# A fused adaLN, linear-attention and SwiGLU block: later modulation rows on VectorE instead of TensorE

## The chip, the cores and the metric

The kernel runs on one core of a Trainium2 chip. The metric is the device time of one execution in microseconds (us), the median over several runs. All times below are in us unless marked ns.

A core has a matrix engine (TensorE, PE in the profile, with its weight loads shown apart as PEld), a vector engine (VectorE, DVE), a scalar engine for activations (ScalarE, ACT), a general engine (GpSimd, POOL) and an engine that issues transfers (SyncE, SP). Each executes its own instructions in order and waits on semaphores for the others. Matmul results land in PSUM, everything else on the chip lies in SBUF.

## The reference

One transformer block whose layer norms are modulated by a condition vector `c`. Six rows of 1024 values come from `c`: shift, scale and gate for the attention half (`sa`, `ca`, `ga`) and for the feed-forward half (`sb`, `cb`, `gb`).

```python
mod = (silu(c) @ w_mod).reshape(1, 6, 1, -1)
sa, ca, ga, sb, cb, gb = (mod[:, k] for k in range(6))

h = layernorm(x) * (1 + ca) + sa                    # x: 2048 x 1024
q, k, v = split(h @ wqkv)                           # 32 heads of 32
pq, pk = phi(q), phi(k)                             # where(t > 0, t + 1, exp(t)) + 1e-6
kv, z = sum_s pk^T v, sum_s pk                      # per head
o = (pq @ kv) / (pq @ z + 1e-6)
x = x + ga * (o @ wo)
h = layernorm(x) * (1 + cb) + sb
x = x + gb * ((silu(h @ w_gate) * (h @ w_up)) @ w_down)   # hidden size 3584
```

Data is bf16 with sums in f32.

## The kernel before

The 2048 tokens are worked in four chunks of 512 (`sc` 0 to 3), each of four tiles of 128 tokens. Work that isn't named below as ordered by hand is put in order by a scheduler at build time; matmuls keep the order of the program.

**Start.** `sa` and `ca` are needed first. Their columns 0 to 767 are summed on TensorE as rows (`mod_rows_a`, called once for each pair of the eight input blocks of `w_mod`), the rest as columns (`mod_cols_b`). Between these TensorE runs matmuls whose result nobody reads (`keep_warm`), so that it stays busy. Chunk 0's tiles are transposed on TensorE.

**Attention, chunk by chunk.** A k phase has eight groups of eight 128x512 matmuls (`k_phase`), a v phase eight more (`v_phase`), a q phase eight (`q_phase`). A k or q group ends with `phi_to`: an exponential on ScalarE, then two VectorE instructions (lines 290 and 292); a v group ends with a copy on ScalarE (line 327). These groups share four PSUM accumulators (pool `pa`), so that a fifth group starts only when the first is evacuated. Another four (pool `pb`) serve all else. After the first two k groups of a chunk come the KV sums of the chunk before (`kv_phase`, tile `kvp` on the chain): 128 small matmuls.

**The next chunk's input.** During chunk `sc` the layer norm of chunk `sc + 1` is made (`ln1`): statistics on VectorE (218 to 210), `rstd` by a power on GpSimd (212), `nmr` on GpSimd (226), the normalised tile `xn` on ScalarE (228), and a transpose by DMA into `hT` from the SP queue (256). When all four tiles are there, eight VectorE instructions modulate `hT` (`modulate_all`, 231), one for each block of 128 columns, and the next k phase reads them in that order.

**The later rows.** `ga`, `sb` and `cb` come in the middle of chunks 2 and 3. `mod_load` loads 1 MB blocks of `w_mod` (tiles `wml`), `ga_rows` and `mod_rows` contract each with silu(c) in 32 matmuls (tile `modr`), ScalarE copies the row, and GpSimd's queue sends it to DRAM and back: `ga` as a broadcast over partitions, `sb` and `cb` as columns (`mod_spread`). `ga` is multiplied into `wo` (553), which VectorE does when the blocks of `wo` are there. `gb` is made otherwise: `gb_sum` multiplies each block by its per-partition factor and adds on VectorE (366, 368), and GpSimd sums over the partitions (`partition_all_reduce`, 703).

**After the chunks.** The q phases of chunks 1 to 3 follow. Between them stand the last KV sums, a transpose of them (`tpk`), the denominators of chunk 0 (`den_sum`, sent out by `den_spread`) and the folding of KV into `wo` (`fold_wo`, four calls of 16 matmuls, two evacuations on ScalarE and two on VectorE). Then the output tiles of chunk 0 (`wo_tile`: two accumulations, the residual, the second layer norm and its transposed `h2T`), and the feed-forward half (`gate_up`, `down`), which takes three quarters of the time; the output tiles of later chunks lie among it.

What the change touches on the queues: SP issues loads and transposes in one order; GpSimd issues the small transfers and computes every `rstd`.

Of the kernel before, what the change touches and what calls it, by code (L numbers as in the profile page):

```python
# [9 lines left out]
ALU = mybir.AluOpType  # L10
# [11 lines left out]
def kernel(  # L22
# [241 lines left out]
    def mod_rows_a(k):  # L264
        for j in range(k * MP, (k + 1) * MP):
            rows = wma[k][:, j % MP, :, :].rearrange("p q (i r) -> p i q r", r=P)
            for g in range(4):
                mm(mod_ps[32 * g:32 * g + 32, 0:A * 64], lhsT=sc32[:, j, :], rhs=rows[:, :, :, 32 * g:32 * g + 32],
                   start=False, stop=(j == DC - 1))
# [38 lines left out]
    def k_phase(sc, lo, hi):  # L308
        if lo == 0:
            pks[sc] = big("pk", [STC, D])  # L310
        for g in k_groups[lo:hi]:
            accs = [acc_a()]
            k_mms(sc, [g], accs)
            k_evac(sc, [g], accs)

# [13 lines left out]
    def q_phase(sc, lo=0, hi=DC):  # L329
        if lo == 0:  # L330
            pqs[sc] = big("pq", [HG, SCW])
        for qc in range(lo, hi):
# [4 lines left out]
            phi_to(pqs[sc][:, qc, :], acc[:])  # L337

# [31 lines left out]
    def ga_rows(blks):  # L370
        ps = acc_b("modr")
        H2 = NB // 2
        for j in range(DC):
            for g in range(4):
                mm(ps[32 * g:32 * g + 32, 0:H2], lhsT=sc32[:, j, :], rhs=blks[g // 2][:, j, (g % 2) * H2:(g % 2 + 1) * H2],
                   start=(j == 0), stop=(j == DC - 1))
        row = small.tile([P, NB], BF16, name="mrow", bufs=1)
        nc.scalar.copy(out=row[:, 0:H2], in_=ps[:, 0:H2])
        for g in range(4):
            nc.gpsimd.dma_start(out=mrow_dram[0, g:g + 1, 0:H2], in_=row[32 * g:32 * g + 1, 0:H2])  # L380
        nc.gpsimd.dma_start(out=ga_bc.rearrange("p (g n) -> p g n", g=4),
                            in_=mrow_dram[0, :, 0:H2].unsqueeze(0).to_broadcast([P, 4, H2]))

    gb_rows = []

    def mod_load(cols):
        blks = []
        for lo in cols:
            t = big("wml", [DC, NB])
            nc.sync.dma_start(out=t[:], in_=wm_v[:, :, lo:lo + NB])  # L390
            blks.append(t)
        return blks

    def mod_rows(blks):
        ps = acc_b("modr")
        for j in range(DC):
            for g in range(4):
                mm(ps[32 * g:32 * g + 32, :], lhsT=sc32[:, j, :], rhs=blks[g][:, j, :],
                                 start=(j == 0), stop=(j == DC - 1))
# [349 lines left out]
```

## Time and profile before

| | |
|---|---|
| median of 3 runs | 836.31 (836.17 to 836.62) |
| profiled execution | 836.56, its span 834.7 |
| TensorE busy | 828.2, 99% of the span |
| VectorE busy | 317.6, 38% |
| ScalarE busy | 168.6, 20% |
| GpSimd busy | 67.5, 8% |
| first v group starts | 30.24, waits 0.31 for `wv` landing |
| KV sums start | 61.95, 90.84, 120.82, 151.65 |
| output tiles of chunk 0 start | 177.09 |
| denominators of chunks 1 to 3 start | 221.98 |

A profile is one execution recorded by the hardware. The span runs from its first to its last instruction. A timeline row has the start, the time taken, the engine, the line of the kernel, the operation and its operands, written out<-in, with shapes; in brackets stands how long the engine had been idle before it and what ended that. A group of instructions merged into one row ends with `x` and their number. The chain that ended last is followed back from the last instruction, at each step to what released it; here it runs through TensorE for 95% of the span.

TensorE executes a 128x512 matmul every 0.217 in a long run (27.73 for 128), though each takes 0.379 from start to end.

### The profile page before, as it was taken

The numbers are of one execution on the slowest core, as the hardware profiler recorded it, in microseconds if no ns is written. First come the engines' busy times: TensorE is split into PE (matmuls) and PEld (weight loads), VectorE is DVE, ScalarE is ACT, GpSimd is POOL, SyncE is SP. The second block draws the span as 40 slices with busy tenths as digits, with TensorE's granted clock in tenths as the row PEclk, the third lists the DMA queues.
The fourth block names the chain that finished last, engine by engine and source line by source line (L and its number), as shares of the span: only waits on it lengthen the run. The fifth ranks groups of instructions, "written<-read, shape, count | busy, mean of one in ns | idle before, by whom it ended". The sixth has DMA issues, their size and how long they took to land.

```text
span 834.7 us, 11272 instructions
## 1 busy us (share of the span) xinstructions
PE 828.2 (99%) x4641; PEld 378.6 (45%) x4641; DVE 317.6 (38%) x606; ACT 168.6 (20%) x253; POOL 67.5 (8%) x168
## 2 busy tenths in 40 slices
PE   8999999999999999999999999999999999999998
PEld 3444444444444444444444444444444444444444
DVE  5755643587344335522222244211114431111122
ACT  3455443334211111101111110111110101111000
POOL 2101201111130201100000010000001100000000
PEclk9999999999999999999999999999999999999999
DMA  9873790129998644636434183662505529710011
GB/s 325 293 202 88 227 194 1 34 61 290 359 247 265 190 151 144 185 117 219 144 114 138 44 227 95 220 221 82 171 1 155 162 69 332 239 53 1 19 58 51
DMA packets 125748, 129.07 MB, mean 155 GB/s; under 512 B 34112, under 2 KB 106304, under 8 KB 125184
## 3 DMA queue, kind: packets, MB, share of 16 engines
q1 hardware_dynamic: 121440, 114.97, 45.7%
q0 software_dynamic: 3968, 12.99, 5.4%
q8 instruction: 36, 0.59, 0.3%
q10 hardware_dynamic: 288, 0.40, 0.1%
q14 instruction: 16, 0.13, 0.1%
HBM read 108.27 MB, written 12.72 MB: 145 GB/s over the span
## 4 chain that ended last, share of the span: by engine, by line
PE 95%; DMA 3%; SPq 1%; DVE 0%; issue 0%; ACT 0%
PE acc L98 88%; PE a_ps L98 7%; DMA wv<-in_A_wqkv_dram 1%; DMA x_sb<-in_A_x_dram 1%; DMA wme<-in_w_mod_dram 1%; PE kvp L98 1%; SPq L140 0%; PE modr L98 0%; PE den L98 0%; SPq L120 0%; DVE wo L577 0%; PE wf L98 0%; SPq L137 0%; DVE pq L292 0%; ACT eb L289 0%
## 5 line engine op out<-in xcount | busy, mean ns | idle before, releaser
L98 PE MATMUL acc<-h2T,wgu 128*128 128x512 bf16 x1792 | 387.6, 379 | 0.0
L98 PEld LDWEIGHTS <-wgu 128*128 128x128 bf16 x1792 | 175.3, 98 | 211.3
L98 PE MATMUL acc<-wd,gu 128*128 128x512 bf16 (+2 forms) x924 | 196.1, 373 | 0.0
L646 DVE TENSOR_TENSOR gu<-acc,e 128x512 bf16<-128x512 f32 x112 | 77.5, 692 | 289.9 <-PE acc L98 289.9
L645 ACT ACTIVATE e<-acc 128x512 f32<-128x512 f32 x112 | 66.9, 597 | 374.8 <-PE acc L98 374.8
L98 PEld LDWEIGHTS <-gu 128*128 128x128 bf16 x924 | 89.3, 98 | 104.5
L98 PEld LDWEIGHTS <-hT 128*128 128x128 bf16 x512 | 49.6, 98 | 60.0 <-issue 1.4
L667 DVE TENSOR_TENSOR e<-acc,gb_bc 128x512 f32<-128x512 f32 (+2 forms) x33 | 22.3, 675 | 131.5 <-PE acc L98 128.6
L98 PE MATMUL a_ps<-wo,pq 128*128 128x512 bf16 x256 | 57.4, 379 | 0.0
L98 PE MATMUL acc<-wk,hT 128*128 128x512 bf16 x256 | 57.1, 379 | 0.0
L98 PE MATMUL acc<-hT,wq 128*128 128x512 bf16 x256 | 56.8, 379 | 0.0
L98 PE MATMUL acc<-wv,hT 128*128 128x512 bf16 x256 | 56.1, 379 | 0.3 <-DMA wv<-in_A_wqkv_dram 0.3
L289 ACT ACTIVATE eb<-acc 128x512 bf16<-128x512 f32 x64 | 37.8, 596 | 74.1 <-PE acc L98 71.0
L228 ACT ACTIVATE xn<-x,nmr,rstd 128x1024 bf16<-128x1024 f32 x16 | 19.8, 1240 | 126.2 <-POOL nmr L226 126.2
L614 POOL DMA_DIRECT2D x_scratch<-x x16 | 9.9, 616 | 377.3 <-DVE x L607 377.3
L98 PEld LDWEIGHTS <-pq 128*128 128x128 bf16 x256 | 25.1, 98 | 30.2
L98 PEld LDWEIGHTS <-wq 128*128 128x128 bf16 x256 | 24.6, 98 | 29.8 <-issue 0.9
L290 DVE TENSOR_SCALAR eb<-eb 128x512 bf16<-128x512 bf16 x64 | 18.5, 294 | 49.4 <-ACT eb L289 49.3
L607 DVE TENSOR_TENSOR x<-a_ps,x_sb 128x512 f32<-128x512 f32 x32 | 22.1, 691 | 7.8 <-PE a_ps L98 7.7
L212 POOL TENSOR_TENSOR rstd<-veps,neg_half 128x1 f32<-128x1 f32 x32 | 17.9, 560 | 80.9 <-DVE veps L210 70.8
L327 ACT CAST v<-acc 128x512 bf16<-128x512 f32 x32 | 18.2, 582 | 23.2 <-PE acc L98 23.2
L670 DVE TENSOR_TENSOR ob<-e,x1r 128x512 bf16<-128x512 f32 (+2 forms) x33 | 22.3, 676 | 1.0
(82 smaller groups left out, 274.6 us busy)
## 6 DMA issues: line engine op xcount, KB each, us to landing
wgu<-in_B_w_gate_dram SPq DMA_DIRECT2D x28, 1024.0 KB, 7.3
wgu<-in_B_w_up_dram SPq DMA_DIRECT2D x28, 1024.0 KB, 8.8
x_sb<-in_A_x_dram SPq DMA_DIRECT2D x32, 256.0 KB, 7.2
x_scratch<-x POOLq DMA_DIRECT2D x16, 512.0 KB, 3.1
x1r<-x_scratch SPq DMA_DIRECT2D x31, 256.0 KB, 2.8
wd<-in_B_w_down_dram SPq DMA_DIRECT2D x7, 1024.0 KB, 7.3
wml<-in_w_mod_dram SPq DMA_DIRECT2D x6, 1024.0 KB, 9.0
rbc<-rden_scratch POOLq DMA_DIRECT2D x16, 256.0 KB, 9.3
```

The lines of the kernel that those rows point to most:

```text
L98: return tc.keep_in_program_order(nc.tensor.matmul(out, lhsT=lhsT, rhs=rhs, start=start, stop=stop))
L212: nc.gpsimd.tensor_tensor(out=rstd[:, 0:n], in0=veps[:, 0:n], in1=neg_half[:].to_broadcast([P, n]), op=ALU.pow)
L228: nc.scalar.activation(out=dst, in_=src, func=ACT.Identity, bias=nmr[:], scale=rstd[:, 0:1])
L289: nc.scalar.activation(out=e[:], in_=acc, func=ACT.Exp)
L290: nc.vector.tensor_scalar(out=e[:], in0=e[:], scalar1=1.0, scalar2=PHI_EPS, op0=ALU.min, op1=ALU.add)
L327: nc.scalar.copy(out=v[:, t * D + nb * NB:t * D + (nb + 1) * NB], in_=acc[:])
L607: nc.vector.tensor_tensor(out=x1[:, ns], in0=a_ps[:], in1=x_t[:, ns], op=ALU.add)
L614: nc.gpsimd.dma_start(out=x1_dram[st * P:(st + 1) * P, :], in_=x1[:])
L645: nc.scalar.activation(out=sg[:], in_=ps[0][:], func=ACT.Silu)
L646: gm = nc.vector.tensor_tensor(out=guT[sc][f // GPT][:, f % GPT, :], in0=ps[1][:], in1=sg[:], op=ALU.mult)
L667: nc.vector.tensor_tensor(out=yt, in0=y_ps, in1=gb_bc[:, ns], op=ALU.mult)
L670: nc.vector.tensor_tensor(out=ob, in0=yt, in1=x1r, op=ALU.add)
```

## The change

Three things are changed.

First, the rows of `ga`, `sb` and `cb` are contracted on VectorE, as `gb` is. `mod_begin` loads a row's two 1 MB blocks and lists 16 steps; `mod_step` takes steps off the list, each of them one VectorE instruction on 128x512 (the first of each half a tensor_scalar, the others a scalar_tensor_tensor that adds into an f32 tile). The calls put 4 steps among chunk 0's q groups, 4, 6 and 8 among the first k groups of chunks 1 to 3 (`K_STEPS`), 6, 6 and 12 ahead of the modulations or behind the v groups (`V_STEPS`), and 2 behind a q group of chunk 1. GpSimd then sums each row over partitions (`mod_total`): `ga` in chunk 2, between its k groups and the layer norm of chunk 3; `sb` at the end of chunk 3; `cb` after `den_spread` of chunk 0. `ga` needs no more DMA; `sb` and `cb` go by DRAM as before. The multiplication of `ga` into `wo` moves behind chunk 3's v groups. The loads of `wml` move: the first two ahead of chunk 1's transposes, and one row's two loads among the four transposes of chunk 2 and of chunk 3. In GpSimd's order a code configuration stands ahead of `ga`'s sum, and another ahead of the first `rstd` of chunk 3.

Second, the denominators of chunk 0 use an accumulator of pool `pa` and stand directly ahead of the first `fold_wo`, the transpose of KV comes one q group earlier, and the four folds lie two q groups apart each.

Third, at the start most of the unread matmuls become 32-bit ones on 256 columns, four in place of eight 512-column bf16 ones, and one of the last group is left out; the last pair of row blocks is summed for the scale in one pass and for the shift in another.

```diff
-    def mod_rows_a(k):
+    def mod_rows_a(k, qs=slice(0, 2), last=True):
...
+                mm(acc[gr, :, qs, :], lhsT=sc32[:, j, :], rhs=rows[:, :, qs, gr], start=False, stop=last and j == DC - 1)
@@ k_phase
             k_evac(sc, [g], accs)
+            mod_step(int(k_groups.index(g) < K_STEPS[sc]))
@@ q_phase
             phi_to(pqs[sc][:, qc, :], acc[:])
+            mod_step(steps)
@@
-    def ga_rows(blks):
-    def mod_load(cols):
-    def mod_rows(blks):
-    def mod_spread(k, row):
...
+    def mod_begin(q):
+        acc = x1p.tile([P, D], F32, name="x1")
+        for half in range(2):
             t = big("wml", [DC, NB])
+            nc.sync.dma_start(out=t[:], in_=wm_v[:, :, q * D + half * NB:q * D + (half + 1) * NB])
+            mod_steps.extend((acc[:, half * NB:(half + 1) * NB], t, j) for j in range(DC))
+        return acc
+
+    def mod_step(n):
+        if n == 0:
+            return
+        with tc.issue_after(last_phi[0].ins):
+            for _ in range(n):
+                acc, t, j = mod_steps.pop(0)
+                if j == 0:
+                    nc.vector.tensor_scalar(out=acc, in0=t[:, 0, :], scalar1=scf[:, 0:1], scalar2=None, op0=ALU.mult)
+                else:
+                    nc.vector.scalar_tensor_tensor(out=acc, in0=t[:, j, :], scalar=scf[:, j:j + 1], in1=acc,
+                                                   op0=ALU.mult, op1=ALU.add)
+
+    K_STEPS = [0, 4, 6, 8]
+    V_STEPS = [0, 6, 6, 12]
+
+    def mod_total(dst, acc):
+        nc.gpsimd.partition_all_reduce(dst, acc[:], P, bass_isa.ReduceOp.add)
+
+    def mod_row(k, acc):
+        row_t = ep.tile([P, NB], F32, name="e")
+        row = row_t[:].bitcast(BF16)
+        mod_total(row, acc)
+        nc.gpsimd.dma_start(out=mrow_dram[k:k + 1, :], in_=row[0:1, :])
+
+    def mod_cols():
...
@@ start
-    keep_warm(spare, 9)
+    keep_warm_f32(spare, 4)
+    keep_warm(spare, 1)
...
-        keep_warm(spare, 5)
-        mod_rows_a(3)
-        keep_warm(spare, 4)
+        keep_warm_f32(spare, 2)
+        keep_warm(spare, 1)
+        mod_rows_a(3, slice(1, 2), False)
+        mod_rows_a(3, slice(0, 1))
+        keep_warm(spare, 3)
@@ chunks
             if sc == 2:
-                ga_rows(blks)
-            if sc == 3:
-                mod_spread(1, mod_rows(blks))
+                mod_total(ga_bc, rows[2])
             k_phase(sc, 4, 8)
...
+        if sc == 0:
+            rows[2] = mod_begin(2)
         v_phase(sc)
...
-            q_phase(0, 0, 6)
+            q_phase(0, 0, 3)
+            q_phase(0, 3, 5, 2)
+            q_phase(0, 5, 6)
+        elif sc + 1 < NSC:
+            rows[sc + 2] = mod_begin(sc + 2)
+        else:
+            mod_row(0, rows[3])
+        if sc + 1 == NSC:
+            with tc.issue_after(last_phi[0].ins):
+                for cc in range(DC):
+                    w = wo[cc // 4][:, cc % 4, :]
+                    nc.vector.tensor_tensor(out=w, in0=w, in1=ga_bc, op=ALU.mult)
+        mod_step(V_STEPS[sc])
         if sc + 1 < NSC:
             with tc.issue_after(last_phi[0].ins):
                 modulate_all(hTs[sc + 1], ca1T, saT)
@@ after the chunks
+    q_phase(1, 2, 3)
+    (transpose of KV)
+    q_phase(1, 3, 4)
+    den_sum(0, acc_a())
+    fold_wo(0, 0)
+    spread = den_spread(0)
+    with tc.issue_after(spread.ins):
+        mod_row(1, rows[4])
+        cols = mod_cols()
     q_phase(1, 4, 6)
-    fold_wo(0, 0)
+    fold_wo(0, 1)
     q_phase(1, 6, 8)
-    fold_wo(0, 1)
+    fold_wo(1, 0)
     q_phase(2, 0, 2)
-    fold_wo(1, 0)
+    fold_wo(1, 1)
     q_phase(2, 2, 3)
-    fold_wo(1, 1)
...
     q_phase(2, 6, 8)
+    with tc.issue_after(last_phi[0].ins):
+        nc.vector.tensor_copy(out=sbT[:], in_=cols[:, 0:DC])
+        nc.vector.tensor_scalar_add(out=cb1T[:], in0=cols[:, DC:2 * DC], scalar1=1.0)
     q_phase(3, 0, 5)
```

## The prediction

> **What bounds the kernel now.** I read the page first, then the chain that ended last in order of time, then the timelines of VectorE, GpSimd (POOL) and the SyncE queue (SP) in the attention stage.
>
> The page's engine line and, from the chain, the stretch between the KV sums of chunks 0 to 3 (start us, us, what):
>
> ```profile
> PE 828.2 (99%) x4641; PEld 378.6 (45%) x4641; DVE 317.6 (38%) x606; ACT 168.6 (20%) x253; POOL 67.5 (8%) x168
> ...
> 61.95 1.15 PE kvp L98 x128
> 63.11 27.73 PE acc L98 x128
> 90.84 1.15 PE kvp L98 x128
> 91.99 3.56 PE acc L98 x16
> 95.55 0.99 PE modr L98 x32
> 96.54 24.28 PE acc L98 x112
> 120.82 1.15 PE kvp L98 x128
> 121.97 3.56 PE acc L98 x16
> 125.53 1.84 PE modr L98 x32
> 127.37 24.28 PE acc L98 x112
> ```
>
> TensorE is the chain: whatever it no longer computes is saved, and whatever makes it wait is lost. So the second question is who could be late. VectorE's timeline, where it modulates hT for the next chunk (in brackets: idle before, and what ended it), and one of its two-tensor steps:
>
> ```profile
> 84.39 2.68 DVE L231 TENSOR_SCALAR hT<-hT,sca 128x512 bf16<-128x512 bf16 x8 [6.52 <-DMA hT<-xn]
> 111.69 2.67 DVE L231 TENSOR_SCALAR hT<-hT,sca 128x512 bf16<-128x512 bf16 x8 [5.38 <-DMA hT<-xn]
> 238.85 2.60 DVE L368 SCALAR_TENSOR_TENSOR x<-x_sb,scf,x 128x1024 f32<-128x1024 bf16 x2
> ```
>
> Both modulations wait for the last transpose. Chunk 2's k groups start 3.47 before the KV sum at 90.84, at 87.37; its first modulation ends near 84.8. Chunk 3's start at 117.35, against 112.1. So hT has a slack of 2.6 and 5.2.
>
> GpSimd, around its only reduce over partitions, with VectorE's veps row and GpSimd's configuration row:
>
> ```profile
> 269.75 6.13 POOL L703 PARTITION_ALL_REDUCE gb_bc<-x  x1 [23.39 <-DVE x L368]
> 316.94 0.58 POOL L614 DMA_DIRECT2D x_scratch<-x  x1 [39.48 <-DVE x L607]
> 325.11 0.59 POOL L212 TENSOR_TENSOR rstd<-veps,neg_half 128x1 f32<-128x1 f32 x1 [7.58 <-DVE x L607]
> 317.65 0.15 DVE L210 TENSOR_SCALAR veps<-mv 128x1 f32<-128x1 f32 x1
> L212 POOLq MODIFY_POOL_CONFIG  x2: 37/37/37, 317.6 to 317.6; - x2
> ```
>
> This rstd had its veps at 317.80 and started at 325.11; the others of these tiles follow theirs in 0.1 to 0.2. The difference is the configuration ahead of it: after a reduce, GpSimd needs about 7.6 (317.52 to 325.11) before it computes rstd again. Here nobody waited for it.
>
> The SP queue, a transpose behind a 1 MB load, with its time to landing; the line after it is the same view of the hT transposes at 73 to 82, which had none ahead:
>
> ```profile
> 328.86 0.79 SPq L631 DMA_DIRECT2D wgu<-in_B_w_gate_dram  x1
> 329.74 2.24 SPq L617 DMA_TRANSPOSE h2T<-xn  x1
> DMA to landing us min/median/max: 6.4/6.4/6.4
> DMA to landing us min/median/max: 3.1/3.6/3.6
> ```
>
> **The change, part by part.** The sum is made against the profiled execution, 836.56 (span 834.7, 1.86 around it), 0.25 above the median of 836.31.
>
> *Row matmuls removed.* The stretch from one KV sum to the next holds 128 full matmuls each time: 27.73 without row matmuls, 28.83 (91.99 to 120.82) and 29.68 (121.97 to 151.65) with. So 1.10 + 1.95 = 3.05 goes, of which 2.83 is the matmuls and the rest the turns between shapes. The two row copies on ScalarE (0.37, 0.59), eight small DMAs and ga's broadcast on GpSimd go too, beside other work.
>
> *Steps added on VectorE.* 48: 6 tensor_scalar and 42 scalar_tensor_tensor on 128x512. By half the L368 row (1.28 for 128x1024) and the L292 row (0.69 for 128x512 from PSUM) I take 0.66 each, and 0.39 (half of 0.745, L366) for the first of each half: 30 us. VectorE has room for the sum (38% busy), so what matters is what queues behind a step.
>
> *Chunk 1.* Four steps among the phi of q groups 3 to 5 (2.3) in front of the modulation at 56.65; VectorE idles 0.71 per group there, so the modulation comes some 1.2 later, and the first k group of chunk 1, due at 58.48, ends 0.3 late. Two more 1 MB row loads lie ahead of chunk 1's transposes, which land by 52.2 and are used at 56.65: hidden unless they lose over 4.
>
> *Chunk 2.* Four k steps and two v steps, 3.7, stand ahead of the last veps (77.72); about 1.4 of that falls into idle time, so it comes 2.3 later, and xn's end (80.2) at 82.5. Its transpose is queued right behind a 1 MB row load that the change puts between the transposes on SP. By the nearest row it takes 6.4, by the undisturbed ones 3.6; I take 6.4, the row with a 1 MB load ahead. It lands at 89.0 (86.2). The eight modulations (2.68) pace the first k group, which ends 3.0 after the landing: 92.0 (89.2) where 89.4 was due (87.37 + 0.3 + 1.73). Loss 2.6 (0).
>
> *Chunk 3.* Here is the new chain. The KV sum starts at 93.7. The last step of ga's row follows the second k group's phi: 92.53 was 1.69 after the KV sum, plus 0.66, gives 96.1. The reduce (its own code is loaded well before: GpSimd gets there after chunk 2's last nmr, near 82) runs to 102.3. But chunk 3's four rstd are queued behind it: plus 7.6, 109.9, where before the first stood at 100.03. xn starts 0.99 later (325.11 to 326.10), ends at 112.1; and in ScalarE's order the v copies stand behind the xn, one by one. TensorE has used its four accumulators for v by 93.7 + 1.15 + 10.40 + 6.93 = 112.2 and waits 0.5 for the first copy (0.58, 112.7). Three more pairs of copy and xn at 1.72: the last xn ends at 117.3, its transpose, again right behind a row load, lands at 123.7 (6.4) or 120.5 (3.2). The first k group ends 3.0 later, at 126.7 (123.5), where 112.7 + 6.93 + 1.73 = 121.4 was due: 5.3 (2.1). Loss 5.8 (2.6).
>
> [...]
>
> *Chunk 3's v groups.* Twelve steps (7.7) and the eight wo multiplications (2 x 2.5, moved here) fill the 12.85 for which VectorE sat idle before 150.59. They come out even, and four accumulators (6.9) cover a delay of q's phi: zero.
>
> *First denominator sums beside the first fold.* A fold costs 0.46 on the chain (160.59 to 164.52 is 3.93 against 3.47 for 16 matmuls), 0.36 of it matmuls: one turn fewer saves 0.10. The four folds now lie two q groups apart; the fourth followed after one and lost 0.69 (168.46 to 171.80 is 3.34 against 2.65). Against it: the KV transposes come after one q group instead of two, with two steps ahead of VectorE's KVB copy (+0.3), and the second fold's evacuation behind the reciprocal (0.95) and the first's (+0.2). Together -0.3, between -0.8 and +0.5.
>
> *Start.* One no-op less (0.2) and the last pair split saves nothing: the wait for wv (landing at 31.54) only grows from its 0.31. Loads up to wv are unchanged. For 32-bit no-ops there is no row; in length they are bounded by the row of 256-column matmuls (0.27) and twice the 512-column one (0.76), and the nine of them replace eighteen of 0.38: at worst no change. Zero.
>
> *Late.* sb's and cb's rows now arrive by a reduce near 172 and two DMAs (1.5 and 4.8): 179, used after 200. The configuration then delays the first rstd of the output tiles by 7.6 (182.59 to 190); the fourth, at 192.95, some 2. h2T is used at 204.59 and the fourth transpose came at 195.3. Zero.
>
> Sum: -3.05 + 0.3 + 2.6 + 5.8 - 0.3 = +5.35, so 841.9, and 841.7 on the median's footing.
>
> **Rivals.**
> *Nothing is late enough (not slower).* One mechanism: the transposes land in 3.6 and 3.2 although a row load stands ahead, because the load is spread over engines and queues. Then chunk 2 loses nothing and chunk 3 2.6: -0.45, 835.9. For it: wo loads of 256 KB ahead of a transpose at 104.23 cost only 5.2. Against it: 6.4. It decides at a landing of about 3.8: above, each us counts twice. If GpSimd's code came back as fast as the 0.30 idle at its first configuration at 1.4 us, chunk 3 would lose nothing as well: 833.3.
> *VectorE held by the reduces (slower still).* Beside the one reduce of the trace only VectorE instructions with an operand in PSUM ran, at 0.68 to 0.69, so it is not shown how one with both operands in SBUF fares; bounds 0 to 6.13 for each reduce. Of the three new ones the second has v copies alone around it; the first would push chunk 3's statistics up to 3 past the rest of the chain, the third the folds by up to 5. Up to +8, half of it 845.7.
> [...]
> *The row matmuls stay hidden in TensorE's time.* Excluded: two stretches differ by them on the chain.
>
> **How the numbers follow.** Chain late as summed: 0.60 (838 to 846). VectorE held as well: 0.20 (845 to 850). Transposes not delayed: 0.13 (834.8 to 837.5). Gain stands: 0.07 (833.3). A measurement of this kernel tells 0.2% (1.7 us) from no change. Slower is the first two and a little of the third, 0.83; same 0.08; faster 0.09. The range leaves out the last case, the lower half of the third and the top of the second: 836.0 to 849.0. The likeliest case alone is 838 to 846.
>
> **What would show it.** Right: waits of a full matmul on hT's modulation near 88 and 122, of v's accumulators on ScalarE near 112; an rstd of chunk 3 some 7.5 after a reduce; transposes of 5 to 7 behind wml; no modr; kvp to kvp 27.7 where nothing waits. Wrong: chunk 3's rstd before 105, transposes at 3.5, VectorE instructions of several us beside a reduce, or a start that ends later than 31.6.

## The result, and the profile after

The changed kernel takes 862.51 (median of 4 runs, 860.92 to 865.08) against 836.3: 1.0316 times the time before, with an interval of 1.0288 to 1.0343. The direction was right, but 862.5 lies far outside the range given, 836 to 849. The profiled execution is the slowest of the four (865.08, span 863.3), so its differences below add up to 28.6 (865.08 − 836.56), not to 26.2.

The engine lines of the page after, and the shares of the chain by engine:

```profile
PE 833.1 (97%) x4505; PEld 381.8 (44%) x4584; DVE 358.0 (41%) x654; ACT 167.3 (19%) x251; POOL 84.8 (10%) x164
...
PE 88%; DVE 7%; issue 2%; DMA 1%; ACT 1%; POOL 0%; DVEq 0%; POOLq 0%; ACTq 0%
```

TensorE is busier than before although it has fewer matmuls, and it is still the engine that ends last. So two things happened: TensorE waited, and its matmuls took longer. To see where, cut both profiles at the same five events: the four KV sums, and the first output tile of chunk 0. The columns are the stretch, its length and the busy time (instructions) of PE, PEld, DVE, ACT and POOL, then the granted TensorE clock, the DMA share and GB/s. Before:

```profile
61.95:90.84 28.89, 28.89 (x266) 13.58 (x269) 15.77 (x41) 13.77 (x20) 3.25 (x8) 1.00 0.54 149
90.84:120.82 29.98, 29.98 (x298) 14.24 (x301) 17.52 (x44) 13.91 (x21) 6.40 (x14) 1.00 0.84 196
120.82:151.65 30.83, 30.83 (x298) 14.24 (x301) 11.35 (x24) 10.04 (x17) 3.32 (x6) 1.00 0.06 15
151.65:177.09 25.44, 25.21 (x323) 11.52 (x324) 19.78 (x41) 11.14 (x20) 4.04 (x8) 1.00 0.19 45
```

After:

```profile
62.07:95.03 32.96, 30.99 (x261) 13.87 (x268) 23.18 (x53) 13.76 (x20) 4.08 (x9) 0.95 0.48 129
95.03:133.48 38.45, 31.20 (x262) 13.79 (x268) 25.31 (x51) 13.57 (x20) 11.56 (x9) 0.96 0.53 120
133.48:170.54 37.06, 31.59 (x262) 14.19 (x268) 27.25 (x41) 9.46 (x16) 7.09 (x3) 0.91 0.17 40
170.54:205.54 35.00, 28.87 (x320) 12.56 (x324) 27.76 (x48) 11.24 (x20) 11.71 (x11) 0.85 0.17 32
```

Every stretch is longer: by 4.07, 8.47, 6.23 and 9.56, together 28.33. The start adds 0.12, and from the first output tile to the end nothing changes (657.76 against 657.6). The third column from the end, the granted clock, shows something new: before, it is 1.00 in all four stretches, after it falls to 0.85. VectorE is busy for at most 27.76 of 35.00 in a stretch; in windows of 5 it has no idle time from 105 to 115 and from 160 to 170.

What TensorE waited for between 28 and 240 (total, times, longest). Before, the same view has nothing above 0.3:

```profile
PE acc L98 <- DVE hT L231: 6.9, 2, 5.1
PE acc L98 <- issue: 5.3, 6, 4.4
PE tp L101 <- DVE kvs L574: 3.6, 1, 3.6
PE acc L98 <- DVE pk L293: 2.0, 4, 0.8
PE wf L98 <- DVE wo L586: 1.8, 2, 1.6
PE acc L98 <- ACT v L329: 0.7, 1, 0.7
```

These are 20.3. In windows of 5, the share of the clock that was not granted, times 5, sums to 12.0 between 60 and 205 (before: 0.0); weighted with TensorE's busy share of each window it is 9.3, so 9.3 to 12.0 went to matmuls at a lower clock. Against that stand the 3.05 of row matmuls and about 0.9 for denominators and folds. 20.3 + (9.3 to 12.0) − 4.0 is 25.6 to 28.3: of the 28.33, all but 2.7 at most is accounted for. Three pieces of the chain after (start us, us, what), and the KV sum ahead of the last:

```profile
82.67 6.14 DMA hT<-xn
...
121.04 6.53 DMA hT<-xn
...
133.48 1.15 PE kvp L98 x128
...
135.39 4.43 issue
```

Three kinds of thing stand on the chain that were not there before: transposes (6.14, 6.53) that land late; an idle 4.43 that waits for nothing the profile shows; and four VectorE instructions of 1.5 to 4.4 whose usual length is 0.3 to 0.5. These four have a common neighbour. GpSimd's timeline and then VectorE's, in the changed kernel:

```profile
97.52 6.13 POOL L402 PARTITION_ALL_REDUCE e<-x  x1 [16.09 <-DVE x L395]
110.71 0.60 POOL L212 TENSOR_TENSOR rstd<-veps,neg_half 128x1 f32<-128x1 f32 x1 [7.06 <-DVE veps L210]
152.97 6.13 POOL L402 PARTITION_ALL_REDUCE e<-x  x1 [18.10 <-DVE x L395]
189.98 6.07 POOL L402 PARTITION_ALL_REDUCE e<-x  x1
```
```profile
98.68 3.52 DVE L291 TENSOR_SCALAR eb<-eb 128x512 bf16<-128x512 bf16 x1 [0.96 <-ACT eb L290]
102.84 1.08 DVE L393 TENSOR_SCALAR x<-wml,scf 128x512 f32<-128x512 bf16 x1
153.35 4.43 DVE L393 TENSOR_SCALAR x<-wml,scf 128x512 f32<-128x512 bf16 x1
157.70 1.54 DVE L291 TENSOR_SCALAR eb<-eb 128x512 bf16<-128x512 bf16 x1
190.80 3.81 DVE L291 TENSOR_SCALAR eb<-eb 128x512 bf16<-128x512 bf16 x1 [0.71 <-ACT eb L290]
```

Each of the four began inside one of the three sums over partitions; outside the sums no tensor_scalar of these lines is long. The ends repeat: 102.20 is 4.68 after the sum's start, 157.78 is 4.81 after it, 194.61 is 4.63 after it. The next tensor_scalar is held again: in the second sum it ended at 159.24, where the sum ended at 159.10; in the first, the step begun at 102.84 took 1.08 instead of 0.48 and ended at 103.92, where the sum ended at 103.65. So a sum of 6.13 holds such an instruction for its first 4.6 to 4.8, and the first two sums hold the next one to their end.

### The profile page after: what moved, and what is told of

It reads as the page before. It is cut to its first block, busy times and chain, and to the rows that moved or that the text cites. A ratio compares the mean times of both kernels' runs of the same rounds, so it can differ in the third digit from the quotient of the medians.

```text
span 863.3 us, 11124 instructions
## 1 busy us (share of the span) xinstructions
PE 833.1 (97%) x4505; PEld 381.8 (44%) x4584; DVE 358.0 (41%) x654; ACT 167.3 (19%) x251; POOL 84.8 (10%) x164
## 4 chain that ended last, share of the span: by engine, by line
PE 88%; DVE 7%; issue 2%; DMA 1%; ACT 1%; POOL 0%; DVEq 0%; POOLq 0%; ACTq 0%
PE acc L98 81%; PE a_ps L98 6%; DVE x L395 2%; DMA hT<-xn 1%; DVE eb L291 1%; DVE stats L218 1%; DVE pk L293 1%; DVE x L393 1%; DVE wo L555 1%; ACT xn L228 0%; ACT eb L290 0%; PE kvp L98 0%; POOL rstd L212 0%; PE mod_ps L98 0%; DVE pq L293 0%
## 5 line engine op out<-in xcount | busy, mean ns | idle before, releaser
L98 PE MATMUL acc<-wk,hT 128*128 128x512 bf16 x251 | 63.2, 408 | 11.8 <-DVE hT L231 6.9
L98 PE MATMUL acc<-hT,wq 128*128 128x512 bf16 x248 | 58.9, 394 | 0.9 <-issue 0.6
L291 DVE TENSOR_SCALAR eb<-eb 128x512 bf16<-128x512 bf16 x64 | 26.3, 415 | 36.6 <-ACT eb L290 36.5
L395 DVE SCALAR_TENSOR_TENSOR x<-wml,scf,x 128x512 f32<-128x512 bf16 x42 | 30.4, 748 | 0.2
```

Of the source, the lines that this page charges most:

```text
L98: return tc.keep_in_program_order(nc.tensor.matmul(out, lhsT=lhsT, rhs=rhs, start=start, stop=stop))
L291: nc.vector.tensor_scalar(out=e[:], in0=e[:], scalar1=1.0, scalar2=PHI_EPS, op0=ALU.min, op1=ALU.add)
L395: nc.vector.scalar_tensor_tensor(out=acc, in0=t[:, j, :], scalar=scf[:, j:j + 1], in1=acc, op0=ALU.mult, op1=ALU.add)
```

## The experiments

The theory (A) after this reading: VectorE has room for the 48 steps; the time is lost because single events come late and TensorE, which has no slack here, passes each delay on. The events are the three sums that hold VectorE, the transposes behind 1 MB loads, GpSimd's return from a sum to `rstd` (7.58 in the profile before), and the idle place behind a KV sum; the lower clock follows the waits. The rival (B): the steps themselves are too much for VectorE around the k groups, and all else is a consequence.

### The sums left out

```diff
             if sc == 2:
-                mod_total(ga_bc, rows[2])
+                (ga_bc filled with ones by GpSimd at the start)
@@ mod_row
-        mod_total(row, acc)
+        nc.gpsimd.memset(row[0:1, :], 0.0)
```

> The changed kernel without its three new sums over partitions on GpSimd: the attention gate's row is set to ones and the other two rows to zeros, so their values are left out; the 48 VectorE steps, the loads, the small transfers and everything else stay. Theory A (the sums are the main cause: they delay the statistics of chunk 3 through GpSimd's return to rstd, and hold VectorE's tensor_scalar for 3.5 to 4.4 us each): the last transpose of chunk 3 lands near 117 instead of 127.6, no tensor_scalar takes over 1 us, and of the 28.5 us lost up to the output tiles only chunk 2's 4.1 and 1 to 3 of VectorE's queue stay: 838 to 843. Theory B (VectorE is simply overloaded by 30 us of steps): 852 or more. Theory C (transposes behind 1 MB loads): 850 to 856, since these stay.

Measured: 850.51, 1.0171 (1.0154 to 1.0187), so 12.0 less than the whole change. All waits of TensorE in this kernel between 28 and 240:

```profile
PE acc L98 <- DVE hT L231: 6.7, 2, 4.5
PE acc L98 <- issue: 5.3, 6, 4.5
```

All four lines behind a VectorE or ScalarE evacuation are gone. The 64 executions of line 291 show why, first after, then without the sums (shortest, median and longest in ns):

```profile
L291 DVE TENSOR_SCALAR eb<-eb x64: 275/292/3815, 28.3 to 237.3; 128x512 bf16<-128x512 bf16 x64
```
```profile
L291 DVE TENSOR_SCALAR eb<-eb x64: 275/293/296, 28.0 to 222.3; 128x512 bf16<-128x512 bf16 x64
```

The longest falls from 3815 to 296. What stays is hT and the idle place, untouched: the last transpose, still behind a load, took 6.66 and landed at 124.10, not near 117. So 850.5 misses theory A's range and lies in theory C's: the sums are the largest single part, 12.0, and far from all. The run does not separate what the sums cost by holding VectorE from what they cost by keeping GpSimd from rstd.

### Fewer steps

The first of these two leaves out 42 of the 48 steps, the second 36, and keeps GpSimd's order as in the whole change by a hand-set order.

```diff
@@ mod_step, 42 left out
-                else:
-                    nc.vector.scalar_tensor_tensor(...)
@@ mod_step, 36 left out
-                else:
+                elif j == DC - 1:
                     nc.vector.scalar_tensor_tensor(...)
@@ with 36 left out, the sums of ga and sb stay behind the last nmr
+        with tc.issue_after(last_nmr[0].ins): mod_total(ga_bc, rows[2])
```

> The changed kernel with only the first step of each half row (6 instead of 48 VectorE steps): the later 42 contractions are left out, so the rows' values are wrong; loads, the three sums on GpSimd and everything else stay. Theory A: chunk 2's wait goes (4.1), chunk 3 still gets its statistics some 7 us after the sum and its transposes behind loads, the held tensor_scalar fall on a VectorE with room: 840 to 848. Theory B: nothing is left but the gain: 833 to 836. Theory C: half of the loss stays, 845 to 850.

> The changed kernel with the first and the last step of each half row alone (12 instead of 48 VectorE steps; the 36 steps between are left out, so the rows' values are wrong). The sums on GpSimd stay behind the same statistics as in the changed kernel and wait for the same last steps; the loads stay between the transposes. Theory A (sums, transposes behind loads, and the clock after each wait): chunk 2's statistics come 2 us earlier, so its 4.1 mostly goes; chunk 3's transposes stay late by 2 to 5, with what follows them; the held tensor_scalar of 3.5 to 4.6 us fall on a VectorE without a queue and cost little: 846 to 853. Theory B (VectorE overloaded by the steps): 834 to 840.

Measured: 875.8, 1.0477 (1.0454 to 1.0500), and 854.4, 1.0219 (1.0203 to 1.0234). The first went the wrong way for both theories, for a reason outside them: with rows ready early, the scheduler placed each of two sums between the third and fourth rstd of a chunk. GpSimd at the first:

```profile
84.00 6.13 POOL L402 PARTITION_ALL_REDUCE e<-x  x1 [6.57 <-issue]
97.47 0.59 POOL L212 TENSOR_TENSOR rstd<-veps,neg_half 128x1 f32<-128x1 f32 x1 [7.35 <-issue]
```

6.57 of idle ahead of the sum, 6.13 for it, 7.35 behind: 20 between two neighbouring rstd, and TensorE waited 15.9 and 16.8 for hT. At the second the idle times are 6.94 and 7.00. It is no test of the steps, but it measures GpSimd's change from a power to a sum and back, since these waits end on nothing that the profile shows. In the second kernel, with a quarter of the steps, TensorE still waited 4.9 for hT, 3.5 at the idle place and 2.7 for the folds. Leaving out the 36 steps gains 8.1, while 18.1 over the kernel before is there without them; at 854.4 it is 1.4 above theory A's range and far from theory B's.

### The loads behind the transposes

```diff
@@ mod_begin of chunks 1 and 2
-            nc.sync.dma_start(out=t[:], in_=wm_v[...])
+            with tc.issue_after(last transpose of the chunk):
+                nc.sync.dma_start(out=t[:], in_=wm_v[...])
```

> The changed kernel with the 1 MB loads of the last two rows issued behind the four transposes of chunks 2 and 3 instead of between them. Theory A: the last transpose of each chunk takes 3 to 4 us instead of 6.1 and 6.5, so chunk 2's wait of 1.8 with its slow clock (4.1 in all) goes and chunk 3's wait of 5.1 falls to about 2; the loss behind chunk 3 stays: 854 to 859. Theory B: no change, 860 to 865. Theory C: 845 or less.

Measured: 853.6, 1.0202 (1.0186 to 1.0217), 8.9 less than the whole. The hT transposes between 80 and 130, times to landing, in this kernel, and as they are with the loads between them (the kernel without sums, whose loads lie as in the change):

```profile
DMA to landing us min/median/max: 3.1/3.3/3.6
```
```profile
DMA to landing us min/median/max: 3.2/3.7/6.7
```

Chunk 2's wait is gone and chunk 3's falls from 5.08 to 2.10, and the time is 0.4 below theory A's range. The load of 1 MB costs the transpose queued behind it about 3 (6.7 at most against 3.6), as the prediction took it. The idle place is not what was gained: 4.43 behind chunk 3's KV sum became 2.48 there and 1.66 behind chunk 2's.

### The idle place behind a KV sum

The 4.43 "issue" at 135.39 lies two matmuls behind the KV sum at 133.48, and no semaphore ends it. Two readings lead on. The page after counts 36 packets, 0.59 MB, for a queue named instruction (q8), 16 KB a packet. If these are pieces of TensorE's instructions, its 4,584 weight loads on that page and as many matmuls, 9,168, make about 255 a piece, by estimate. And in this window the DMA engines are full (87.1% of their time goes to the loads' queue, q1), with one such packet (40 slices of 134.6 to 140, busy share in tenths):

```profile
DMA  9696999999699996999888797999989986000000
```

The theory (F), an assumption of the author's: a KV sum executes 256 instructions (128 loads, 128 matmuls) in 1.15, faster than a new piece comes over busy DMA engines; if a piece ends shortly behind the sum, TensorE runs dry. Then the place must follow the count of TensorE's instructions, whatever they are. The change's start alone adds 14 (the split pair 16 more; one no-op, an unread matmul with its load, 2 less), so it can be tried on the kernel before. One run has the start alone; one has in it one no-op replaced by eight tiny matmuls (14 instructions more); one three no-ops by 24.

```diff
@@ the kernel before, with the change's start; then in place of one no-op
-    keep_warm(spare, 1)
+    for _ in range(8):
+        mm(spare[0:32, 0:64], lhsT=sel[:, 0, 0:32], rhs=sel[:, 0, 0:64], ...)
@@ or in place of three
-        keep_warm(spare, 3)
+        for _ in range(24): (the same)
```

> The kernel before with only the changed start: 32-bit zero matmuls in place of pairs of 16-bit ones, one fewer, and the last pair of the first rows contracted scale first. By the prediction's step nothing, since the wait for the value weights (landing near 31.5) sets the end of the start: 836.1 to 836.6. Rival (the start moves the end of the start): 0.3 us or more to either side.

> The kernel before with only the changed start, as in the run of the start alone, and one zero matmul of the first group replaced by eight tiny ones (32x64): the places at which TensorE's instruction blocks begin are then within two instructions of those of the kernel before. Theory F (the start alone cost 1.0 because its shorter instruction stream made a block end just behind chunk 1's KV sum, where TensorE idled 1.3 us): no idle there, 836.0 to 836.6. Rival (the start itself costs): 837.0 or more.

> The kernel before with only the changed start, and three zero matmuls of the start (six instructions of TensorE) replaced by 24 tiny ones (48 instructions), so that a block of 256 instructions no longer begins within ten instructions of the end of a KV sum. Theory F (a block that the KV sum's 256 instructions empty in 1.2 us is gone before the next has arrived): no idle behind or in the KV sums, 836.0 to 836.6. Rival (the start costs in another way): 837 or more.

Measured: 837.32, 1.0009 (1.0001 to 1.0018); 837.77, 1.0014 (1.0006 to 1.0023); 836.55, 1.0000 (0.9991 to 1.0009). The chain with the start alone, and with 14 instructions more:

```profile
90.81 1.15 PE kvp L98 x128
91.96 0.97 PE acc L98 x4
92.93 1.32 issue
```
```profile
90.93 1.13 PE kvp L98 x125
92.06 1.06 issue
93.12 0.21 PE kvp L98 x3
```

Four matmuls are 8 instructions behind the sum, three are 6 before its end: the idle place moved by exactly the 14 that were added. So 837.77, a time that speaks for the rival, does not contradict theory F: the shift of 14 was too small to clear the sum. With 42 more the idle place is gone, and so is the cost of the start. The same in the whole change, with 31 tiny matmuls added at the start, 8 in place of one no-op, and 24 in place of three:

> The changed kernel with 31 tiny matmuls (32x64, 62 instructions of TensorE with their weight loads) at its very start, where TensorE waits for the first data; nothing else changes but the places at which TensorE's instruction blocks of 16 KB begin. Theory F (the idle 4.4 us behind chunk 3's KV sum is TensorE waiting for its next block of instructions, which arrived within that gap while the DMA engines were full): the gap moves away or shrinks below 1, and the half clock behind it shortens: 855 to 859. Rival (the gap belongs to chunk 3's data or to the clock): it stays, 861 to 865.

> The changed kernel with the same replacement of one zero matmul by eight tiny ones at the start, which costs no time there. Theory F: no idle of TensorE behind the KV sums that ends on nothing, and none of the half clock that followed it; the idle was 4.4 and the half clock behind it cost some 1.8: 854 to 858. Rival: 861 to 865.

> The changed kernel with the same 24 tiny matmuls in place of three zero matmuls. Theory F: the idle 4.4 behind chunk 3's KV sum and the half clock behind it (1.8) go, the waits for hT, for VectorE and their half clocks stay: 855 to 858. Rival: 861 to 865.

Measured: 859.1, 1.0276 (1.0257 to 1.0295); 863.6, 1.0322 (1.0308 to 1.0336); 859.4, 1.0270 (1.0256 to 1.0284). With 31 and with 24 the idle place is gone, for 3.4 and 3.1 less; with 8 it moved to four matmuls before the sum's end, 3.77 long, and nothing was won. With 31 and 24 the gain is smaller than the 4.43, and the times lie just above theory F's ranges (855 to 859 and 855 to 858): the waits for hT are 8.5 and 9.8 there instead of 6.9. Why they are longer stays open.

That TensorE lacks its instructions there is theory F, and no row shows it. What the runs show is that the place follows the count of TensorE's instructions: in the kernel before with the new start, 14 more move it by 14, and with 42 more, there and in the whole change, or 62 more there is none above 0.2. The idle places measured are 1.1 to 4.5 long and lie in or just behind a KV sum; in the kernel with the start alone the DMA engines are full as well (q1 106.8% from 91.9 to 94.3).

### TensorE kept busy through its waits

```diff
@@ k_phase, ahead of the first k group
+            if sc >= 2: keep_warm(acc_b("warm"), 8 if sc == 2 else 23)
```

> The changed kernel with matmuls on zeros (results unused) put on TensorE's queue ahead of the k groups of chunk 2 (8 of 256 columns, about 1 us) and chunk 3 (23, about 3 us), to fill part of the waits of 1.8 and 5.1 us there. Theory A with the clock (a wait of TensorE of some 2 us or more is followed by a granted clock of 0.5 for 3.4 us or a multiple): the half clock after chunk 2's wait goes, and after chunk 3's if what is left of the wait is under 2; 4 us in all: 857 to 861. Rival (the matmuls behind a wait are slow because the modulations feed them one by one): no change, 861 to 865.

Measured: 851.9, 1.0189 (1.0174 to 1.0204). Unread matmuls make the whole change 10.6 faster, 5 better than theory A's range. They also add to the count of instructions, and the idle place is gone here; so the kernel to compare with is the one with 24 tiny matmuls, which has no idle place either: 859.4, 7.5 more. From the first KV sum to the output tiles it takes 136.6, this one 129.35: the same 7.3. The window of chunk 3's wait in that kernel, then in this one:

```profile
120.00:150.00 30.00, 22.73 (x216) 10.08 (x217) 13.79 (x31) 9.28 (x16) 1.47 (x4) 0.89 0.78 166
```
```profile
120.00:150.00 30.00, 27.62 (x245) 12.53 (x247) 19.22 (x32) 8.21 (x15) 6.44 (x3) 1.00 0.70 148
```

The 31 unread matmuls have 512 columns, not 256 as expected, and fill 6.7 (at 0.217), and the waits for hT are 2.0 instead of 9.8; so the time of waiting is about the same, with something in it. What differs is the clock: 0.89 against 1.00, and 0.94 against 1.00 from 90 to 120. The clock not granted, summed as above, is 8.6 in the one and 1.7 in the other. In the whole change it is 0.66 from 90 to 95, behind the 1.81 of chunk 2, and behind the 4.43 it looks like this:

```profile
140.00:145.00 5.00, 5.00 (x13) 1.79 (x12) 2.23 (x5) 0.60 (x1) 0.00 (x0) 0.50 0.03 7
```

In 140 to 145 TensorE is busy without a gap and executes 13 full matmuls, where 23 fit at 0.217: half the clock is missing.

Read in windows of 0.5, the low clock of the change lies at 90.60 to 94.01, 128.14 to 131.56, 138.38 to 145.21, 175.93 to 182.76 and 196.41 to 199.82. These are pieces of 3.41 or two in a row, and their starts are 11, 3, 11 and 6 times 3.413 apart: in the change they lie on a grid. Each piece at half clock withholds 1.71, so the clock not granted, 12.0, 8.6 and 1.7, makes seven in the change, five in the kernel with 24 tiny matmuls, one in this.

How much of one piece of the grid TensorE waits goes with the clock of the next. In the change, between 55 and 230, the pieces at full clock with 1.66, 1.81, 2.40, 2.99 and 3.42 of waiting were each followed by one at half clock; one with 1.58 and all with less were not. The wait of 1.81 lies whole in one piece (87.19 to 90.60, TensorE busy for 1.60 of 3.41 at a clock of 1.00), and the next has a clock of 0.50. The length of a wait alone does not decide: in the first kernel with all cures below, the 48 matmuls of k groups behind a wait of 2.44 took 12.13, those behind one of 2.87 took 10.58.

### The other two parts alone

The denominators and folds alone, in the kernel before:

```diff
-    q_phase(1, 2, 4)
+    q_phase(1, 2, 3)
     (transpose of KV)
-    den_sum(0)
-    den_spread(0)
+    q_phase(1, 3, 4)
+    den_sum(0, acc_a())
+    fold_wo(0, 0)
+    den_spread(0)
     q_phase(1, 4, 6)
-    fold_wo(0, 0)
+    fold_wo(0, 1)
     (the other two likewise)
```

> The kernel before with only the rearrangement around the folds: the transposes of KV after one q group instead of two, the first denominator sums directly ahead of the first fold and on the accumulators of the big matmuls, the four folds two q groups apart. By the prediction's step: 0.3 less, with bounds of 0.8 less and 0.5 more: 835.5 to 836.8. Theory A (this part is harmless; its loss in the changed kernel comes from VectorE's queue and the third sum): the same. Rival (the part itself makes TensorE wait for KV's copies on VectorE, 3.6 us in the changed kernel): 838 to 841.

Measured: 835.39, 0.9987 (0.9978 to 0.9996): 0.9 less than before, 0.1 below the expected range. Its first fold, and the two q groups behind it:

```profile
156.82 0.36 PE wf L98 x16
157.19 3.56 PE acc L98 x16
```

The other three folds follow in the same way, 0.36 each, and none waits. In the whole change the third sum holds an eb of the q groups there, and the same folds wait 1.8.

### All cures together

The loads behind the transposes and the sums left out as above, all 48 steps in place, and the count of instructions shifted: by 8 tiny matmuls in the first kernel, by 24 in the second.

> The changed kernel with all three cures at once: loads of the last two rows behind the transposes, the instruction blocks shifted as above, and the three sums on GpSimd left out (the gate's row is ones, the other two zeros, so these values are wrong). All 48 VectorE steps stay. If the causes named (transposes behind loads, instruction blocks, sums with GpSimd's returns, and the half clock after each wait) are all there is, the gain of the removed matmuls stands: 832 to 835. Theory B (VectorE overloaded by the steps): 838 or more.

> The changed kernel with loads behind the transposes, without the three sums on GpSimd (the gate's row is ones, the other two zeros, so these values are wrong), and with the 24 tiny matmuls; all 48 VectorE steps stay. Against the run of all three cures (842.2), which kept 5.3 of idle time in its KV sums, 5.3 and some 1.7 of half clock go: 834 to 836.5, with 1.3 still waited for chunk 3's transposes. Theory B (VectorE overloaded by the steps): 840 or more.

Measured: 842.2, 1.0069 (1.0055 to 1.0082), and 839.17, 1.0030 (1.0019 to 1.0042). With 8 the idle place came at both other KV sums (2.44 and 2.87); with 24 there is none. The longest waits left on TensorE in the second (the next line has 0.8, in five pieces):

```profile
PE acc L98 <- DVE hT L231: 3.1, 2, 2.8
```

The three cures alone were worth 12.0, 8.9 and 3.1; their sum, 24.0, would give 838.5, and 839.2 was measured. They are nearly separate losses. With all 48 steps on VectorE no wait of TensorE stands on an evacuation, so theory B does not explain the 26. But theory A is not all either: 842.2 and 839.2 miss its ranges (832 to 835, 834 to 836.5). The steps are not free. From the first KV sum to the output tiles this kernel takes 117.61 (62.01 to 179.62); denominators and folds alone take 114.14, less 3.05 for row matmuls 111.09. Of the 6.5 between, 3.05 are the two waits for hT and 3.1 the 16 matmuls behind them, which take 4.38 and 5.63 instead of 3.46, the second with one piece at half clock (1.7). The last xn of chunk 3 ends at 114.35, 22.2 behind the KV sum at 92.18; with denominators and folds alone it ends 17.3 behind it (107.93 − 90.63). So the steps among the k groups push the statistics of the next chunk back by 4.9. The last transposes of both chunks, with the loads now right behind them, take 4.58 and 4.98 as well, where the kernel with the loads alone moved had at most 3.6.

### The sums moved, nothing left out

The whole change with loads behind the transposes and the count of instructions shifted; `ga`'s and `sb`'s sums moved together into chunk 3's v groups, `cb`'s behind the folds; the last step of `ga` and of `cb` is kept back to stand directly ahead of the sum (left out below).

```diff
@@ chunk 2
-                mod_total(ga_bc, rows[2])
@@ behind chunk 3's v groups
-            mod_row(0, rows[3])
+            with tc.issue_after(last_phi[0].ins):
+                mod_total(ga_bc, rows[2])
+                mod_row(0, rows[3])
@@ behind the folds
+    with tc.issue_after(last_phi[0].ins):
+        mod_row(1, rows[4])
+        cols = mod_cols()
```

> The whole change with the cures and complete results: loads behind the transposes, the 24 tiny matmuls, the sums of the first two rows behind chunk 3's statistics and k groups, the third behind the last fold. Against the run of all cures the sums are back: two in a row hold tensor_scalar on VectorE twice for 4 to 5 us in chunk 3's v groups, where 12 steps and the output weights' multiplications stand already, the third once beside q's phi. If 7 us of accumulators cover them: 834 to 836. If not: 837 to 842. It beats the attention gate's row alone (834.4) only if all of that is hidden.

Measured: 853.6, 1.0201 (1.0187 to 1.0215), far above both ranges. GpSimd, and VectorE behind the first sum:

```profile
141.49 12.63 POOL L413 PARTITION_ALL_REDUCE e<-x  x2 [14.82 <-DVE x L403]
```
```profile
148.03 9.26 DVE L571 TENSOR_TENSOR wo<-wo,e 128x1024 bf16<-128x1024 bf16 x8 [0.69 <-POOL e L413]
```

Moving the sums to where ScalarE evacuates does not help when two stand back to back and VectorE has a queue: a step was held for 4.76, `ga`'s multiplication took 9.26 instead of 4.90, steps stood behind it, and TensorE waited 9.0 for the KV copy.

### Only what stays free

The kernel before with the new order of denominators and folds; only `ga`'s row on VectorE, its steps behind the last nmr of chunks 1 and 2 and one behind each later k group of chunk 3; its sum alone in chunk 3's v groups. `sb` and `cb` stay on TensorE, and so do the loads and the start.

```diff
+        if sc in (1, 2):
+            with tc.issue_after(last_nmr[0].ins):
+                ga_step({1: 6, 2: 4}[sc])
+        if sc == 3:
+            with tc.issue_after(last_phi[0].ins):
+                nc.gpsimd.partition_all_reduce(ga_bc, ga_acc[0][:], P, bass_isa.ReduceOp.add)
+                (ga into wo)
@@ k_phase, behind a group
+            if sc == 3 and k_groups.index(g) >= 2:
+                ga_step(1)
```

> The kernel before with the rearrangement around the folds, and of the rows only the attention gate's on VectorE: its loads where they were, its 16 steps behind the statistics of chunks 2 and 3 and one behind each of chunk 3's last six k groups, its sum on GpSimd in chunk 3's v groups, where VectorE had nothing to do, and the multiplications of the output weights behind it. The other two rows stay on TensorE. If a contraction costs nothing where no statistics, no transpose and no modulation stand behind it, 1.1 less than the rearrangement alone (835.4): 834.0 to 834.8. Rival (the sum still holds up the last k groups or q's phi, or a block of instructions comes late): 836 or more.

Measured: 834.40, 0.9978 (0.9969 to 0.9987): faster than both kernels. The chain between KV sums, and what VectorE does behind the sum of 6.13 at 138.29:

```profile
62.72 27.73 PE acc L98 x128
90.45 1.15 PE kvp L98 x128
91.60 27.73 PE acc L98 x128
```
```profile
144.45 4.90 DVE L544 TENSOR_TENSOR wo<-wo,e 128x1024 bf16<-128x1024 bf16 x8 [6.30 <-POOL e L541]
```

27.73 twice: `ga`'s 1.10 is saved in full. The sum finds VectorE with nothing to do for 6.30; the next longest idle time of VectorE in this kernel's attention stage is 5.62, ahead of chunk 3's modulation.

## Why the prediction was right and wrong

The step that failed is the cost of the three new sums on VectorE: the prediction put it at nothing in its sum and left it to a rival. The runs showed that each sum holds VectorE's tensor_scalar, and leaving the sums out gains 12.0. Two further terms were missing: the lower clock behind a wait, and the idle place at a KV sum. Term by term:

*TensorE is the chain; 3.05 for the row matmuls.* Right: 27.73 for 128 matmuls wherever nothing waits, and 1.10 saved by the last kernel.

*A step takes 0.66, the first of a half 0.39; VectorE has room.* Right in the sum: 0.66 to 0.67 on the chain, and without the late events no evacuation is waited for. The delay that the steps put on chunk 3's statistics, 4.9 without any sum, had no term for chunk 3: there the sum let only the reduce delay them.

*Chunk 1.* Right: 0.1 against 0.3, the start included.

*Chunk 2.* The steps held: landing at 88.81 (89.0), wait and pacing (eight modulations, 2.68, feed eight matmuls that need 1.73) 2.7 (2.6). The stretch still lost 4.07, since its matmuls ran at half clock behind a wait of 1.81. The sum had no term for the clock.

*Chunk 3.* The time of the first rstd was right, 110.71 (109.9), its path only in part. GpSimd's return is real: 7.00 and 7.35 with six steps, and 7.50 with twelve, where the veps had been ready for 3.4. But in the change this rstd started 0.16 behind its veps, the usual distance:

```profile
110.40 0.15 DVE L210 TENSOR_SCALAR veps<-mv 128x1 f32<-128x1 f32 x1
```

VectorE's statistics had become as late as GpSimd, because the first reduce held an eb for 3.52 at 98.68, and through it the statistics. That the two met at one time is luck; without the sums the first rstd stands at 107.11. The runs have 6.57 and 6.94 into the sum and 7.00 to 7.50 back, near the row's 7.6. Of what the prediction calls code, the trace shows a configuration (MODIFY_POOL_CONFIG): for the first sum at 81.4, which then started behind its last step at 97.52 (16.09 idle, ended by VectorE), and for the rstd behind it at 103.6; what GpSimd does in the idle time no row shows. On TensorE 5.8 was forecast, and 9.57 came: 5.08 for hT, 1.9 for four v accumulators and their copies, the rest pacing and clock.

*Chunk 3's v groups: zero.* Wrong. 7.7 of steps and 5 of multiplications fit into 12.85 only if nothing holds them. The second sum held 4.43 + 1.54, the KV copy came late, and TensorE waited 3.62 for it.

*Denominators and folds: −0.3, between −0.8 and +0.5.* Alone −0.9, slightly beyond the better end; in the whole, the third sum turned it into waits of 1.8.

*Start: zero.* Right for its own time, 836.55 once the count of instructions is shifted. Wrong in effect: with 14 instructions more an idle place stood behind a KV sum, 1.0 alone. In the whole change, whose matmul counts move it on to another KV sum, the idle place cost 3.1 to 3.4 net.

*Late: zero.* Right: 657.76 against 657.6.

*The rival of held VectorE*, given 0.20 and up to +8, was the right mechanism. Leaving out the sums is worth 12.0; its bound of 0 to 6.13 each holds what was measured (3.2, 5.2 and 3.5 beyond the usual lengths), but it had no clock behind a wait either. The error was to leave it a rival: a cost with no row nearer than 0 and 6.13 belonged in the sum, and not at its lower end. In the trace a sum does not hold VectorE for its whole length: the hold ends 4.6 to 4.8 into 6.13, and in the first two sums it returns for the next tensor_scalar.

*Transposes not delayed*: excluded by 6.14 and 6.53, against 3.1 to 3.6 with the loads elsewhere.

So the 26.2 are: sums 12.0, loads 8.9, the idle place about 3.1, each with the lower clock that it brought, and some 6.5 that is left with all cures (statistics delayed by the steps, last transposes of 4.6 to 5.0), against 4.0 of gains. The prediction had the loads, GpSimd's return and the gains; it lacked the holds, the idle place and the clock.

## What to carry to other kernels

Where one engine has no slack, work moved to an idle engine is priced by what queues behind it, not by its busy share. Look for every long instruction of a neighbour (here a sum of 6.13 on GpSimd) and ask which short ones of VectorE fall into it. Add to a wait of TensorE the clock that it may lose behind it: in the change 1.7, half a piece of 3.41, behind each piece with 1.66 or more of waiting. When a change elsewhere makes an idle place appear that no semaphore explains, count the instructions from the start: here 42 and 62 more of them removed it, for 3.1 and 3.4 of 862.5.

## What was not expected of the hardware

A few instructions at the start cost 1.0 some 80 us later (1.32 of idle at 92.93), and 42 more bring it back. Unread matmuls in TensorE's waits made a kernel 10.6 faster, some 6.9 of it by the clock and 3.1 by the idle place that they moved away. GpSimd's change is paid in both directions, 6.57 and 6.94 into the sum and 7.00 to 7.50 back to a plain power. In the change the lower clock lies on a grid of 3.41, which speaks for the place of a wait beside its length. What stays open: why a piece with 1.58 of waiting was not followed by half clock and one with 1.66 was, and why the hold of a sum pauses before its end. A two-tensor step in 32 bits took its usual 0.74 at 146.61, during a sum, in the kernel with moved sums; whether it is free of the hold or only hit the pause was not tried. The wait for chunk 2's hT also differs between kernels with the same code there: 1.81, 1.97, 2.63 and 3.44.
